# Sparse attention and FFN on one core: plain f32 loads with casts on the engines, attention spread by slots, a second output buffer, a fixed order for the first batch

## The chip, the cores and the metric

The kernel runs on one core of a Trainium2 chip. The metric is the device time of one execution in microseconds (us). The executions of one kernel that counted as fast agree within 1.5%: an execution further above the fastest of its kernel counts as slow, and fast runs are compared with fast runs alone. A median is of all runs of a kernel.

The engines of the core are TensorE (PE; its weight loads are listed as PEld), VectorE (DVE), ScalarE (ACT), GpSimd (POOL) and SyncE (SP, which here only issues transfers). Sixteen DMA engines move data between DRAM and the on-chip memory (SBUF). TensorE writes its results to PSUM.

The kernel before took 375.92 us (median of 4 runs, 373.97 to 377.35).

## The reference

The first part is an attention over 4 batches and 8 heads of 768 tokens with 64 elements each. A token sees its neighbours at a distance below 16, and beside them one summary of each block of 32 tokens: the maximum of the block's keys and the mean of its values. The second part is a feed-forward network (FFN) on the result, 3072 tokens of 512.

```python
k_sum = k.reshape(B, H, nb, block, D).max(axis=3)         # block = 32
v_sum = v.reshape(B, H, nb, block, D).mean(axis=3)
scores_l = scale * q @ k.T                                # kept where |i - j| < 16
scores_s = scale * q @ k_sum.T + log(block)
a = softmax(concat(scores_l masked, scores_s))
x = a @ concat(v, v_sum)                                  # then to (3072, 512)
h = x @ w_in                                              # 512 -> 2048
g = h * clip(h + 3, 0, 6) / 6
out = g @ w_out                                           # 2048 -> 512
```

(The code is abridged: names of axes and reshapes are left out.)

## The kernel before

The tokens are cut into 8 tiles of 384, two for each batch, and the heads are handled as 4 pairs (p). Stage s of the outer loop runs the attention of half batch s, the first FFN matmul (F1) of tile s-1 and the second (F2) of tile s-2. One stage has 16 slots: four F1 matmuls and three F2 matmuls each, with some steps of the attention in between. The order on TensorE is the program's. The other engines were ordered by the scheduler.

All of k, q, v and the weights came in bf16, by transfers that cast on the way and are issued by GpSimd. Only the rows for the block sums came as f32 from SyncE:

```python
def load_k(b, p):
    t = ld.tile([128, NT, 2, D], BF16, tag="kb", name="kb")
    for j in range(2):
        nc.gpsimd.dma_start(out=t[:, :, j], in_=k[b, 2 * p + j].rearrange("(s p) d -> p s d", p=128))
# ... the same for load_q and load_v, w_in and w_out in four chunks each
```

The transposes of keys and queries share one PSUM buffer. The key's transpose is read by two copies and the block maximum before the query's may overwrite it:

```python
ps_o = ctx.enter_context(tc.tile_pool(name="ps_o", bufs=1, space=PS))   # output of F2
ps_t = ctx.enter_context(tc.tile_pool(name="ps_t", bufs=1, space=PS))   # transposes
# ...
def Tk(b, p):
    tp = ps_t.tile([128, S], BF16, tag="t", name="tk")
    # ... 6 transposes
    nc.scalar.activation(t[0:64, :, 0:64], tp[0:64].rearrange(...), AF.Copy)
    nc.vector.tensor_copy(t[64:128, :, 64:128], tp[64:128].rearrange(...))
    nc.vector.reduce_max(red[:], tp[:].rearrange(...), axis=AX.X)
    nc.vector.tensor_tensor(kst[e][p]..., red..., hmk[:], op=ALU.mult)

def Tq(b, p, lo, hi):
    tp = ps_t.tile([128, S], BF16, tag="t", name="tq")
    # ... the transposes
    nc.vector.tensor_copy(qT[e][p][:, ...], tp[:, ...])
```

The scores are masked after the exponential, on DVE for batch 0 and on GpSimd later. GpSimd also makes the block sums of v for batches 1 to 3. Each half batch is one list of steps, and the even half carries all key work and the block sums of the batch:

```python
eng = nc.vector if b == 0 else nc.gpsimd
eng.tensor_tensor(a, a, mask[:].unsqueeze(1).to_broadcast([128, n, WIN]), op=ALU.mult)
# ...
T(0); T(1); L(0); T(2); L(1); A(0); T(3); L(2); A(1); L(3); A(2); A(3)
```

T stands for the transposes, L for scores and their exponential, A for the value step (numerator, denominator, and x = numerator times exp(-ln(denominator))). One slot of the FFN ends in a relu on ScalarE and a multiply on DVE that writes g:

```python
nc.scalar.activation(r[:], hp[:], AF.Relu, bias=half_c[:], scale=1.0 / 6.0)
nc.vector.scalar_tensor_tensor(gt[t][:, ft], r[:], 1.0, hp[:], op0=ALU.min, op1=ALU.mult)
```

The softmax here doesn't subtract the row's maximum and nothing guards it: scores larger than these inputs give would overflow.

Of the kernel before, what the change touches and what calls it, by code (L numbers as in the profile page):

```python
# [11 lines left out]
U32 = mybir.dt.uint32  # L12
# [5 lines left out]
D = 64  # L18
BLK = 32
# [7 lines left out]
def kernel(  # L27
# [19 lines left out]
    NTILE = B * 2  # L47

# [3 lines left out]
    ld = ctx.enter_context(tc.tile_pool(name="ld", bufs=5))  # L52
    vld = ctx.enter_context(tc.tile_pool(name="vld", bufs=1))
    work = ctx.enter_context(tc.tile_pool(name="work", bufs=2))
    xp = ctx.enter_context(tc.tile_pool(name="xp", bufs=3))
    gp = ctx.enter_context(tc.tile_pool(name="gp", bufs=2))
# [3 lines left out]
    ps_o = ctx.enter_context(tc.tile_pool(name="ps_o", bufs=1, space=PS))  # L60
    ps_t = ctx.enter_context(tc.tile_pool(name="ps_t", bufs=1, space=PS))
# [6 lines left out]
    kbd = [[const.tile([128, NK, 128], BF16, tag=f"kbd{e}{p}", name=f"kbd{e}{p}") for p in range(NP)] for e in range(2)]  # L68
    vbd = [[const.tile([128, NK, 128], BF16, tag=f"vbd{e}{p}", name=f"vbd{e}{p}") for p in range(NP)] for e in range(2)]
    qT = [[const.tile([128, S + 2 * HALO + 2], BF16, tag=f"qT{e}{p}", name=f"qT{e}{p}") for p in range(NP)] for e in range(2)]  # L70
    at = [[const.tile([128, NK, WIN], BF16, tag=f"at{e}{p}", name=f"at{e}{p}") for p in range(NP)] for e in range(2)]
    kst = [[const.tile([128, 128], BF16, tag=f"kst{e}{p}", name=f"kst{e}{p}") for p in range(NP)] for e in range(2)]
    vst = [[const.tile([128, 2, D], BF16, tag=f"vst{e}{p}", name=f"vst{e}{p}") for p in range(NP)] for e in range(2)]
    vfull = [vld.tile([128, BLK, D], F32, tag=f"vf{i}", name=f"vf{i}") for i in range(2)]
# [4 lines left out]
    kb_t, qb_t = {}, {}  # L79

    def load_k(b, p):
        t = ld.tile([128, NT, 2, D], BF16, tag="kb", name="kb")
        for j in range(2):
            nc.gpsimd.dma_start(out=t[:, :, j], in_=k[b, 2 * p + j].rearrange("(s p) d -> p s d", p=128))  # L84
        kb_t[b, p] = t

    def load_q(b, p):
        t = ld.tile([128, NT, 2, D], BF16, tag="qb", name="qb")
        for j in range(2):
            nc.gpsimd.dma_start(out=t[:, :, j], in_=q[b, 2 * p + j].rearrange("(s p) d -> p s d", p=128))  # L90
        qb_t[b, p] = t

    def load_v(b, p):
        t = vbd[b % 2][p]
        for j in range(2):
            nc.gpsimd.dma_start(  # L96
                out=t[j * 64:(j + 1) * 64, :, j * 64:(j + 1) * 64],
                in_=v[b, 2 * p + j].rearrange("(n p) d -> p n d", p=KB))

    def load_vfull(b, g):  # L100
        t = vfull[g]
        for j in range(2):
            src = v[b, 4 * g + 2 * j:4 * g + 2 * j + 2].rearrange("h (n t) d -> (h n) t d", t=BLK)
            nc.sync.dma_start(out=t[j * 64:j * 64 + 2 * NB], in_=src)
# [3 lines left out]


    for p in range(NP):  # L110
        load_k(0, p)
        load_q(0, p)
# [3 lines left out]
    identf = work.tile([128, 128], F32, tag="idf", name="identf")  # L116
    make_identity(nc, identf[:])
    nc.vector.tensor_copy(ident[:], identf[:])  # L118
    obd = const.tile([128, 2, D], BF16, tag="obd", name="obd")
    hmk = const.tile([128, 2, NB], BF16, tag="hmk", name="hmk")  # L120
    for t in (obd, hmk):
        nc.vector.memset(t[:], 0.0)
        nc.vector.memset(t[0:64, 0], 1.0)
        nc.vector.memset(t[64:128, 1], 1.0)

    def zero_off_diagonal(t):
        nc.vector.memset(t[0:64, :, 64:128], 0.0)
        nc.vector.memset(t[64:128, :, 0:64], 0.0)

    for e in range(2):  # L130
        for p in range(NP):
            zero_off_diagonal(kbd[e][p])
            zero_off_diagonal(vbd[e][p])
            nc.vector.memset(qT[e][p][:, 0:HALO], 0.0)
            nc.vector.memset(qT[e][p][:, S + HALO:], 0.0)
            nc.vector.memset(kst[e][p][:], 0.0)
    for g in range(2):
        nc.vector.memset(vfull[g][32:64], 0.0)
        nc.vector.memset(vfull[g][96:128], 0.0)
# [4 lines left out]
    for j in range(2):  # L144
        m = mask[j * 64:(j + 1) * 64]
        nc.gpsimd.affine_select(out=m, in_=m, compare_op=ALU.is_ge, fill=0.0, base=0,
                                channel_multiplier=-1, pattern=[[1, WIN]])
        nc.gpsimd.affine_select(out=m, in_=m, compare_op=ALU.is_ge, fill=0.0, base=2 * HALO,
                                channel_multiplier=1, pattern=[[-1, WIN]])

    hmv, osum = [], []
    for par in range(2):
        m = const.tile([128, 2, D], F32, tag=f"hmv{par}", name=f"hmv{par}")
        nc.gpsimd.memset(m[:], 1.0)
        for j in range(2):
            lo = 64 * par + NB * j
# [4 lines left out]
        o = const.tile([128, 2, D], BF16, tag=f"osum{par}", name=f"osum{par}")  # L161
# [4 lines left out]
    for g in range(2):  # L166
        load_vfull(0, g)
    for p in range(NP):
        load_v(0, p)
    for c in range(4):  # L170
        w = d_ff // 4
        nc.gpsimd.dma_start(out=w_in_sb[:, :, c * w:(c + 1) * w], in_=w_in_v[:, :, c * w:(c + 1) * w])
    for c in range(4):
        w = NFT // 4
        nc.gpsimd.dma_start(out=w_out_sb[:, c * w:(c + 1) * w], in_=w_out_v[:, c * w:(c + 1) * w])


    def vsum(b, g):
        eng = nc.vector if b == 0 else nc.gpsimd
        t = vfull[g]  # L180
        n = BLK // 2
        a = work.tile([128, n, D], F32, tag="va", name="va")
        eng.tensor_tensor(a[:], t[:, 0:n], t[:, n:2 * n], op=ALU.add)  # L183
        while n > 1:
            n //= 2
            eng.tensor_tensor(a[:, 0:n], a[:, 0:n], a[:, n:2 * n], op=ALU.add)  # L186
        for par in range(2):
            eng.tensor_tensor(vst[b % 2][2 * g + par][:], a[:, 0:1].to_broadcast([128, 2, D]), hmv[par][:], op=ALU.mult)
        if b + 1 < B:
            load_vfull(b + 1, g)  # L190


    asum, nd = {}, {}

    def Tk(b, p):
        e = b % 2
        src = kb_t[b, p][:].rearrange("p s h d -> p s (h d)")
        tp = ps_t.tile([128, S], BF16, tag="t", name="tk")
        for st in range(NT):
            nc.tensor.transpose(tp[:, st * 128:(st + 1) * 128], src[:, st], ident[:])  # L200
        t = kbd[e][p]
        nc.scalar.activation(t[0:64, :, 0:64], tp[0:64].rearrange("p (n c) -> p n c", c=KB), AF.Copy)  # L202
        nc.vector.tensor_copy(t[64:128, :, 64:128], tp[64:128].rearrange("p (n c) -> p n c", c=KB))
        red = work.tile([128, NB], BF16, tag="red", name="red")
        nc.vector.reduce_max(red[:], tp[:].rearrange("p (n c) -> p n c", c=BLK), axis=AX.X)  # L205
        off = 64 * (p % 2)
        nc.vector.tensor_tensor(
            kst[e][p][:, off:off + 2 * NB].rearrange("p (h n) -> p h n", h=2),
            red[:].unsqueeze(1).to_broadcast([128, 2, NB]), hmk[:], op=ALU.mult)

    def Tq(b, p, lo, hi):
        e = b % 2
        src = qb_t[b, p][:].rearrange("p s h d -> p s (h d)")
        tp = ps_t.tile([128, S], BF16, tag="t", name="tq")
        for st in range(lo, hi):
            nc.tensor.transpose(tp[:, (st - lo) * 128:(st - lo + 1) * 128], src[:, st], ident[:])  # L216
        nc.vector.tensor_copy(qT[e][p][:, HALO + lo * 128:HALO + hi * 128], tp[:, 0:(hi - lo) * 128])

    def Sl(b, p, lo, hi):
        e = b % 2  # L220
        n = hi - lo
        sp = ps_s.tile([128, 512], F32, tag="s", name="sl")
        for i in range(n):
            t = lo + i
            nc.tensor.matmul(sp[:, i * WIN:(i + 1) * WIN], kbd[e][p][:, t], qT[e][p][:, t * KB:t * KB + WIN],  # L225
                             start=True, stop=True)
        a = at[e][p][:, lo:hi]
# [4 lines left out]
    def Ss(b, g, half):  # L232
        e = b % 2
        sp = ps_s.tile([128, 512], F32, tag="s", name="ss")
        for par in range(2):
            p = 2 * g + par
            nc.tensor.matmul(sp[:, 0:HALF], kst[e][p][:], qT[e][p][:, HALO + half * HALF:HALO + (half + 1) * HALF],
                             start=(par == 0), stop=(par == 1))
        a = work.tile([128, HALF], BF16, tag="asum", name="asum")
        nc.scalar.activation(a[:], sp[:, 0:HALF], AF.Exp, scale=scl)  # L240
# [11 lines left out]
    def AVn(b, p, half):  # L252
        e = b % 2
        num = ps_n.tile([128, HALF], F32, tag="num", name="num")
        nd[b, p, half] = [num, None]
        bl = blocks_of(half)
        nc.tensor.matmul(num[:], vst[e][p][:].rearrange("p h d -> p (h d)"), asum[b, p // 2, half][:],  # L257
                         start=True, stop=False)
        for i, (t, lo, hi, off) in enumerate(bl):
            nc.tensor.matmul(num[:, lo:hi], vbd[e][p][:, t], at[e][p][:, t, off:off + hi - lo],  # L260
                             start=False, stop=(i == len(bl) - 1))

    def AVd(b, p, half, x):
        e = b % 2
        den = ps_n.tile([128, HALF], F32, tag="den", name="den")
        num = nd[b, p, half][0]
        a = at[e][p]
        ones = obd[:].rearrange("p h d -> p (h d)")
        nc.tensor.matmul(den[:], osum[p % 2][:].rearrange("p h d -> p (h d)"), asum[b, p // 2, half][:],
# [87 lines left out]
    for stage in range(NTILE + 2):  # L357
# [3 lines left out]
        if stage == 0:  # L361
            for st in steps:
                st()
# [44 lines left out]
```

## Time and profile before

| what | value |
|---|---|
| median of 4 runs | 375.92 us |
| profiled span | 376.5 us |
| PE busy | 255.8 us (68%) |
| DVE, ACT, POOL busy | 158.8, 157.2, 152.5 us (42, 42, 41%) |
| first FFN matmul | 65.9 us |
| TensorE's largest single wait on another engine after that | 16.2 us, for a mask on GpSimd |

The three engines beside TensorE are equally and lightly loaded on average, so averages tell little here. What matters is the table by stages, which the prediction below shows line by line: the start, the even stages, the tail. Its rows are cut at the first relu of each tile, except the first, which is cut at the first FFN matmul (66 us; the first relu is at 68.3).

### The profile page before, as it was taken

The numbers are of one execution on the slowest core, as the hardware profiler recorded it, in microseconds if no ns is written. First come the engines' busy times: TensorE is split into PE (matmuls) and PEld (weight loads), VectorE is DVE, ScalarE is ACT, GpSimd is POOL, SyncE is SP. The second block draws the span as 40 slices with busy tenths as digits, with TensorE's granted clock in tenths as the row PEclk, the third lists the DMA queues.
The fourth block names the chain that finished last, engine by engine and source line by source line (L and its number), as shares of the span: only waits on it lengthen the run. The fifth ranks groups of instructions, "written<-read, shape, count | busy, mean of one in ns | idle before, by whom it ended". The sixth has DMA issues, their size and how long they took to land.

```text
span 376.5 us, 4613 instructions
## 1 busy us (share of the span) xinstructions
PE 255.8 (68%) x1696; PEld 143.2 (38%) x1696; DVE 158.8 (42%) x336; ACT 157.2 (42%) x297; POOL 152.5 (41%) x203
## 2 busy tenths in 40 slices
PE   0000257886670179898857798989477989899985
PEld 0000234453340135454424454545244545454432
DVE  7475852465461042433454334334543343343310
ACT  1000234476250035556615455656254656564421
POOL 8992102899999933276334032520020302200000
PEclk9999999999798559999978899999788999999999
DMA  9999999997997660197763001900000000001011
GB/s 76 92 107 191 187 183 203 146 136 109 133 145 69 42 42 30 34 106 72 70 40 25 28 30 31 89 28 17 13 0 30 29 29 29 28 14 43 30 56 56
DMA packets 83990, 26.51 MB, mean 70 GB/s; under 512 B 76032, under 2 KB 80128, under 8 KB 83200
## 3 DMA queue, kind: packets, MB, share of 16 engines
q0 software_dynamic: 79488, 13.64, 47.5%
q1 hardware_dynamic: 4480, 12.59, 14.2%
q8 instruction: 13, 0.21, 0.3%
q14 instruction: 9, 0.07, 0.1%
HBM read 33.55 MB, written 6.29 MB: 106 GB/s over the span
## 4 chain that ended last, share of the span: by engine, by line
PE 54%; POOL 16%; ACT 10%; DMA 9%; DVE 6%; issue 4%; POOLq 0%; ACTq 0%
PE hp L334 21%; PE op L348 20%; DMA wout<-in_moe_w_out_dram 9%; POOL vbd L96 3%; POOL va L186 3%; ACT ot L352 3%; POOL qb L90 3%; POOL kb L84 3%; POOL va L183 2%; DVE red L205 2%; PE num L260 2%; PE num L257 2%; ACT kbd L202 2%; PE sl L225 2%; PE tq L216 2%
## 5 line engine op out<-in xcount | busy, mean ns | idle before, releaser
L348 PE MATMUL op<-wout,g 128*128 128x512 bf16 x384 | 110.8, 399 | 13.9 <-ACT ot L352 13.7
L334 PE MATMUL hp<-x,win 128*128 128x384 bf16 x512 | 115.3, 351 | 1.6 <-DVE g L338 0.8
L338 DVE SCALAR_TENSOR_TENSOR g<-r,hp 128x384 bf16<-128x384 f32 x128 | 70.7, 553 | 103.6 <-ACT r L337 103.0
L337 ACT ACTIVATE r<-hp,half_c 128x384 f32<-128x384 f32 x128 | 73.8, 577 | 85.4 <-PE hp L334 83.5
L230 POOL TENSOR_TENSOR at<-at,mask 128x376 bf16<-128x376 bf16 (+2 forms) x36 | 30.2, 843 | 105.7 <-ACT at L228 105.7
L334 PEld LDWEIGHTS <-win 128*128 128x128 bf16 x512 | 48.5, 104 | 30.5 <-issue 8.2
L348 PEld LDWEIGHTS <-g 128*128 128x128 bf16 x384 | 39.4, 103 | 49.2 <-issue 20.1
L216 PE MATMUL tq<-ident,qb 128*128 128x128 bf16 x96 | 12.8, 255 | 55.1 <-DVE red L205 53.2
L284 DVE TENSOR_TENSOR x<-num,lg 128x384 bf16<-128x384 f32 x32 | 17.9, 558 | 59.1 <-ACT lg L283 59.0
L90 POOL DMA_DIRECT2D qb<-in_q_dram x32 | 27.0, 864 | 31.7 <-PE tq L216 19.5
L84 POOL DMA_DIRECT2D kb<-in_k_dram x32 | 27.2, 867 | 27.5 <-DMA win<-in_moe_w_in_dram 12.4
L228 ACT ACTIVATE at<-sl 128x376 bf16<-128x376 f32 (+2 forms) x48 | 22.9, 483 | 27.0 <-PE sl L225 26.7
L282 ACT ACTIVATE lg<-den 128x384 f32<-128x384 f32 x32 | 15.6, 489 | 43.7 <-PE den L277 36.1
L216 PEld LDWEIGHTS <-qb 128*128 128x128 bf16 x96 | 7.9, 110 | 63.3 <-issue 61.0
L202 ACT ACTIVATE kbd<-tk 64x768 bf16<-64x768 bf16 x16 | 12.8, 802 | 43.9 <-PE tk L200 43.5
L260 PEld LDWEIGHTS <-vbd 128*128 128x128 bf16 x224 | 13.9, 104 | 32.6 <-issue 27.6
L260 PE MATMUL num<-at,vbd 128*128 128x94 bf16 (+2 forms) x224 | 15.1, 210 | 16.3 <-POOL at L230 16.3
L96 POOL DMA_DIRECT2D vbd<-in_v_dram x32 | 24.6, 781 | 3.7 <-DMA wout<-in_moe_w_out_dram 3.5
L200 PE MATMUL tk<-ident,kb 128*128 128x128 bf16 x96 | 10.0, 254 | 20.1 <-DVE ident L118 15.8
L352 ACT ACTIVATE ot<-op 128x512 f32<-128x512 f32 x24 | 14.2, 592 | 11.6 <-PE op L348 11.2
L225 PEld LDWEIGHTS <-kbd 128*128 128x128 bf16 x192 | 15.0, 115 | 9.9 <-issue 4.0
L225 PE MATMUL sl<-qT,kbd 128*128 128x94 bf16 x192 | 17.9, 231 | 0.0
(63 smaller groups left out, 233.7 us busy)
## 6 DMA issues: line engine op xcount, KB each, us to landing
vf<-in_v_dram SPq DMA_DIRECT2D x16, 384.0 KB, 7.5
out_dram<-ot SPq DMA_DIRECT2D x24, 256.0 KB, 2.0
kb<-in_k_dram POOLq DMA_DIRECT2D x32, 96.0 KB, 3.4
qb<-in_q_dram POOLq DMA_DIRECT2D x32, 96.0 KB, 3.4
vbd<-in_v_dram POOLq DMA_DIRECT2D x32, 96.0 KB, 3.4
win<-in_moe_w_in_dram POOLq DMA_DIRECT2D x4, 512.0 KB, 21.3
wout<-in_moe_w_out_dram POOLq DMA_DIRECT2D x4, 512.0 KB, 35.1
```

What stands on the lines that cost most here:

```text
L84: nc.gpsimd.dma_start(out=t[:, :, j], in_=k[b, 2 * p + j].rearrange("(s p) d -> p s d", p=128))
L90: nc.gpsimd.dma_start(out=t[:, :, j], in_=q[b, 2 * p + j].rearrange("(s p) d -> p s d", p=128))
L96: nc.gpsimd.dma_start(out=t[j * 64:(j + 1) * 64, :, j * 64:(j + 1) * 64], in_=v[b, 2 * p + j].rearrange("(n p) d -> p n d", p=KB))
L216: nc.tensor.transpose(tp[:, (st - lo) * 128:(st - lo + 1) * 128], src[:, st], ident[:])
L225: nc.tensor.matmul(sp[:, i * WIN:(i + 1) * WIN], kbd[e][p][:, t], qT[e][p][:, t * KB:t * KB + WIN], start=True, stop=True)
L230: eng.tensor_tensor(a, a, mask[:].unsqueeze(1).to_broadcast([128, n, WIN]), op=ALU.mult)
L260: nc.tensor.matmul(num[:, lo:hi], vbd[e][p][:, t], at[e][p][:, t, off:off + hi - lo], start=False, stop=(i == len(bl) - 1))
L334: nc.tensor.matmul(hp[:], w_in_sb[:, kt, ft * 128:(ft + 1) * 128], xt[t][:, kt], start=(kt == 0), stop=(kt == NP - 1))
L337: nc.scalar.activation(r[:], hp[:], AF.Relu, bias=half_c[:], scale=1.0 / 6.0)
L338: nc.vector.scalar_tensor_tensor(gt[t][:, ft], r[:], 1.0, hp[:], op0=ALU.min, op1=ALU.mult)
L348: nc.tensor.matmul(ops[t][:], gt[t][:, ft, ts * 128:(ts + 1) * 128], w_out_sb[:, ft], start=(ft == 0), stop=(ft == NFT - 1))
L352: nc.scalar.activation(o[:], ops[t][:], AF.Copy)
```

## The change

The intent is to take the issuing of transfers from GpSimd, to break up the serial chains of the even stages, and to start the FFN earlier. Its parts are these.

- All transfers are plain f32, issued by SyncE. The casts to bf16 are instructions on DVE, and on ScalarE for half of the weights and part of the first batch.
- The attention of a whole batch is spread over the 32 slots of two FFN stages. Batch 1 is packed into stages 0 and 1, batches 2 and 3 into stages 2 and 3 and stages 4 and 5. F2 lags F1 by two tiles.
- The transposes lose their own PSUM buffer and take turns in pools of two that others use too; F2's output has two buffers in place of one. In batches 0 and 1 every second numerator and denominator uses the output's buffers (`alt`).
- The first batch has a fixed order on ScalarE, DVE and GpSimd.
- Smaller parts: one set of tiles for the keys, queries, values and exponentials where there was one for even and one for odd batches; one buffer more for x and for g; block sums on 96 rows in place of 128, those of the first batch on GpSimd; for the later batches both copies of a key's transpose on ScalarE; and copies out of the transposes that write every second element.

```diff
-        nc.gpsimd.dma_start(out=t[:, :, j], in_=k[b, 2 * p + j].rearrange("(s p) d -> p s d", p=128))
+    for n, src in (("k", k), ("q", q)):
+        t = ld.tile([128, NT, 2 * D], F32, tag=n + "f", name=n + "f")
+        nc.sync.dma_start(out=t[:], in_=src[b, 2 * p:2 * p + 2].rearrange("h (u p s) d -> p (h u) (s d)", p=128, s=2))
+    ...
+    copy = nc.scalar.copy if b == 0 and n == "q" else nc.vector.tensor_copy
+    copy(t[:, :, :, j], r[:, :, j])
-    ps_o = ctx.enter_context(tc.tile_pool(name="ps_o", bufs=1, space=PS))
-    ps_t = ctx.enter_context(tc.tile_pool(name="ps_t", bufs=1, space=PS))
+    ps_o = ctx.enter_context(tc.tile_pool(name="ps_o", bufs=2, space=PS))
+    alt = b < 2 and p % 2 == 1
+    pool = ps_o if alt else ps_n
-        T(0); T(1); L(0); T(2); L(1); A(0); T(3); L(2); A(1); L(3); A(2); A(3)
+            quad = [(0, lambda p=pa: Tk(b, p)), (1, lambda p=pa: Tq(b, p)),
+                    (2, lambda p=pb: Tk(b, p)), (3, lambda p=pb: Tq(b, p)),
+                    ...
+                    (9, lambda p=pa: AV(b, p, 0)), (11, lambda p=pb: AV(b, p, 0)),
+                    (13, lambda p=pa: AV(b, p, 1)), (15, lambda p=pb: AV(b, p, 1))]
+            steps += [(start + int((o + s) * scale), f) for s, f in quad]
+    start = tc.manual_schedule(engines={ET.Activation, ET.DVE, ET.Pool})
+    ...  (the first batch, in order)
+        start, scale = (8, 0.75) if b == 1 else (32 * (b - 1), 1)
```

(The loads of v and the weights change in the same way.)

## The prediction

> **What bounds the kernel now.** I read first the forty slices, then the busy time stage by stage, then the waits of the slow stages, then the chain that ended last. In the page's slices (a digit is tenths busy, a slice 9.4 us):
>
> ```profile
> PE   0000257886670179898857798989477989899985
> PEclk9999999999798559999978899999788999999999
> DMA  9999999997997660197763001900000000001011
> q0 software_dynamic: 79488, 13.64, 47.5%
> q1 hardware_dynamic: 4480, 12.59, 14.2%
> ```
>
> TensorE does almost nothing for four slices while the DMA engines are full; counted from 0, there is a hole in slices 12 and 13, and the clock falls there and near slices 20 and 28. The last two lines say which queue holds the DMA engines: the casting loads from GpSimd. I cut the span where the first of each 16 relu evictions starts (ScalarE line 337), so each row is one stage of the loop (columns: start:end, length, then busy time of PE, weight loads, DVE, ACT, POOL, then clock, DMA share, GB/s):
>
> ```profile
> 0.00:66.00 66.00, 15.87 (x121) 11.17 (x122) 39.98 (x111) 11.31 (x21) 34.08 (x60) 1.00 1.33 148
> 66.00:91.50 25.50, 21.35 (x151) 12.53 (x149) 14.09 (x29) 15.93 (x32) 23.60 (x29) 1.00 1.49 136
> 91.50:156.30 64.80, 37.45 (x232) 20.35 (x231) 22.77 (x36) 21.61 (x41) 46.26 (x56) 0.76 0.76 70
> 156.30:186.60 30.30, 27.06 (x193) 15.22 (x193) 11.66 (x24) 17.59 (x34) 18.51 (x24) 1.00 0.89 79
> 186.60:232.10 45.50, 34.49 (x232) 19.35 (x232) 19.09 (x36) 21.50 (x41) 11.00 (x14) 0.89 0.25 31
> 232.10:262.40 30.30, 27.05 (x193) 15.21 (x193) 11.65 (x24) 17.57 (x34) 9.02 (x10) 1.00 0.38 47
> 262.40:307.50 45.10, 34.05 (x233) 19.02 (x233) 19.08 (x36) 21.45 (x42) 6.05 (x8) 0.89 0.05 18
> 307.50:337.80 30.30, 27.08 (x193) 15.25 (x193) 11.66 (x24) 17.60 (x34) 3.99 (x4) 1.00 0.08 27
> 337.80:360.00 22.20, 20.54 (x108) 10.51 (x108) 8.31 (x15) 10.21 (x18) 0.00 (x0) 1.00 0.10 37
> 360.00:376.50 16.50, 10.85 (x49) 4.58 (x47) 0.55 (x1) 2.39 (x4) 0.00 (x0) 1.00 0.17 64
> ```
>
> There are three losses: 66 us before the first FFN matmul; even stages of 45 us (the first 65 us) against odd ones of 30 us; and 22 + 16.5 us at the end, where TensorE is the bound. The waits and the chain say why:
>
> ```profile
> PE tq L216 <- DVE red L205: 53.2, 16, 17.7
> PE num L260 <- POOL at L230: 16.3, 2, 16.2
> PE op L348 <- ACT ot L352: 13.7, 17, 0.9
> 27.94 32.92 DMA wout<-in_moe_w_out_dram
> ```
>
> First line: the query transposes wait for the key's reduce, because one PSUM buffer serves both, 16 times. Second: in the 65 us stage the mask multiply stood on GpSimd behind loads and block sums (its timeline there is full from 108 to 130 us), and TensorE waited 16.2 us at once. Third: one output PSUM buffer, some 0.8 us at each of 17 evictions. Fourth: on the chain of the start, 33 us are a weight transfer.
>
> **What the Trainium skill says.** "DMA: Bandwidth & Descriptors", section "SWDGE vs HWDGE vs iDMA": a load that casts must be issued from GpSimd, whose cores make the descriptors; plain ones go from SyncE and take nothing from GpSimd. The trace agrees: 96 K/Q/V issues of some 840 ns are GpSimd time (27.2 + 27.0 + 24.6 us); a SyncE issue of the same size is 0.32 us. "TensorE: Matmul & The Clock Gate", section "Part 1": after idleness the array runs at half clock. Here, four FFN matmuls are 0.81 us in the undisturbed stage but 1.48 us after the 16 us hole. "VectorE: DVE Perf Modes", section "The perf-mode tier table": an fp32 copy between SBUF tiles runs two elements a cycle. No such big copy is in this trace; the bf16 copy from PSUM (561 ns for 768 elements) has that rate. "SBUF — State Buffer", section "Who interferes with whom": such a copy, and a DVE operation with two SBUF inputs, block against GpSimd for a whole instruction. Here the 128x48 multiply that writes kst takes 183 ns in the median and 3895 ns once, with GpSimd busy. The change adds many such copies.
>
> **The change, part by part.**
> (1) Loads. All come from SyncE as f32. Bytes landed rise from 26.5 MB to 40 MB (q, k, v, and v again, 6.29 MB each, 8.4 MB weights, 6.29 MB out), but rows become longer: 512 B for q and k. Rates, as estimates from the page: q0's 79488 packets share 47.5% of 16 x 376.5 us, 36 ns each; q1's 4480 share 14.2%, 191 ns for 2.8 KB, which is 236 GB/s. At 36 ns a packet on 16 engines, 512 B rows give 227 GB/s and 256 B rows (v) 114. Batch 0 in the order of SyncE's queue: q and k 3.15 MB 13.9 us, v rows 1.57 MB 6.7, v 1.57 MB 13.8, first w_in chunk 1.05 MB 4.4: 39 us, and 2.5 for start and landing, 41 us. The chain of compute beside it: ScalarE's fixed list for batch 0 has about 38 instructions at 0.5 to 1.0 us (8 query casts, 8 PSUM copies of 0.8, 12 exponentials of 0.48, 4 vbd casts, logs), 27 us, from 6 us on, plus some 6 us of waits for DVE and TensorE: about 40 us. So the first FFN matmul comes at **43 us in place of 66: -23**.
> (2) Stages 0 and 1 (32 FFN1 slots, rest of batch 0, all of batch 1, no FFN2). ScalarE: 32 relu at 0.65 us (start to start when back to back) 20.8, kbd 8 x 0.80, exponentials 12 x 0.5, sums 6 x 0.5, logs 24 x 0.52, weight casts 7 x about 1.05: 56 us. DVE: 32 x 0.57 for g, 12 x 0.56 for x, 16 q/k casts of 384 at about 0.36, 8 v casts of 768 at 0.56, qT, reduces, weight casts 7 x 0.7: 48 us, and some 6 of blocking. TensorE: about 38 us. DMA has 65 us of work after the first w_in chunk at the rates above (w_in 13.3, batch 1 34.4, w_out 17.8). All are near 55 to 65 in dependent order: **67 us**. Before, the two stages with this FFN1 work took 25.5 + 64.8 = 90.3 us; they held half of batch 1 less, and one FFN2 (48 matmuls at 0.217, 10.4 us) more, which after lies in the tail.
> (3) Stages 2 to 5, two pairs with one batch each. TensorE at full clock: a slot of 4 + 3 matmuls is 1.30 us (the undisturbed stage repeats every 1.29 to 1.30), 32 slots 41.6. Attention of one batch, from start-to-start times in warm stretches: 8 value steps (a head pair's numerator and denominator for one half) x 0.84, 48 score matmuls x 0.04, 8 block-sum scores x 0.16, 48 transposes x 0.055: 6.7 + 1.9 + 1.3 + 2.6 = 12.5. So 54 us. By the durations of (2), ScalarE needs 47 (relu 20.8, kbd 6.4, exponentials 8, logs 8.3, evictions 3.6) and DVE 41 (g 18.2, x 4.5, casts 10.3, qT and reduces 7.6) plus blocking. What goes: the transposes now lie a slot apart and use two buffers, so the 2.5 us wait per head is over other work, and GpSimd has no issues, so no mask waits. What comes: bursts of two kbd copies (1.6 us) or four casts (1.4 us) before a relu or g, while only two hp buffers give about 0.5 to 1 us of slack: about 8 stalls of 1 us. A pair is **62 us, two are 124**; before it was 75.8 and 75.4.
> (4) Stages 6 and 7: pure FFN, 32 x 1.30 = 41.6, with two output buffers no eviction wait: **42.5**.
> (5) Tail: FFN2 lags two stages, so 96 matmuls at 0.217 (16 took 3.63 us, less 0.38 of the last's own latency, by 15) are 20.8; last eviction and store as before, 3.5: **24.3** in place of 16.5.
> Sum: 43 + 67 + 124 + 42.5 + 24.3 = **301**; several terms were rounded upwards, so I put **298 us**.
>
> **Rivals.** *ScalarE and DVE become the bound everywhere*: for it, 87% and 76 to 87% of the ideal pair; against it, evictions can be delayed a little without TensorE stopping. Then pairs cost 70 and stages 0 and 1 75: about 322 us. *DMA becomes the bound of stages 0 and 1*: 40 MB, SyncE's queue in order, so a load waiting for its buffer holds all behind it, and DVE's casts of batch 2 stand before the g of stage 2. For it, the DMA row of before is full to 85 us; against it, no descriptors from GpSimd and 2 KB rows. It would add 10 to 20 us: 310 to 318. *Everything hides*: first matmul at 38, stages 0 and 1 at 56, pairs at 57, 276 us. *The cost only moves, no gain*: this needs 80 us of new stalls; the FFN content, about 166 us at 1.30 per slot, does not change, and nothing speaks for it.
>
> **Range and chances.** The ends of the range are the second and the third rival with small luck: **276 to 322**, eight in ten. Faster by over 2% is below 369.6 us, 70 us away: 0.97. Within 2%: 0.02. Slower: 0.01.
>
> **What would show it.** First FFN matmul at 39 to 47 us; the first FFN2 at 100 to 118; pairs of 57 to 68 us with no wait of TensorE over 3 us and a clock of 0.95 or more after 110 us; no GpSimd issues; 42 to 44 us for the two pure stages; 96 matmuls in one run at the end. I am wrong if the first w_in chunk lands after 50 us, if TensorE's longest waits are for DMA after 60 us, or if relu or g wait queues make pairs of over 70 us.

## The result

The changed kernel took **296.46 us** (median of 4 runs, 294.99 to 298.65) and is correct. Its ratio to the kernel before is 0.789, with a 95% interval of 0.7825 to 0.7963. Ratios here are the mean time of one kernel's fast runs over the mean of the other's fast runs of the same rounds, so they are not quite the ratio of the medians. The profiled execution has a span of 295.4 us, at a mean clock of 0.96.

Slices of the changed kernel, 7.4 us each (digits as before), and its only busy DMA queue:

```profile
PE   0533868749969497799859998999999999999995
POOL 8885000595234019660293075400420000000000
PEclk9999999966999969999986999999999999999999
DMA  8999949992860999664874770011100101001211
q1 hardware_dynamic: 58752, 39.85, 53.5%
```

TensorE starts early and is nearly full from slice 21 on. The queue of casting loads is gone. The DMA row is full at the start, again in slices 13 to 15, and stays half busy up to slice 23. The clock row still dips, now in slices 8 and 9, 14 and 20 to 21.

The stages, cut at the first relu of each tile (columns as in the prediction; the border of stages 0 and 1 lies one relu, some 0.46 us, too early, here and in the stages of the other runs):

```profile
0.00:42.65 42.65, 18.37 (x154) 13.67 (x155) 29.86 (x71) 26.18 (x45) 23.27 (x43) 1.00 0.97 229
42.65:73.04 30.39, 22.66 (x179) 14.33 (x178) 27.00 (x40) 22.67 (x41) 14.40 (x15) 0.83 0.97 220
73.04:98.97 25.93, 21.70 (x203) 13.93 (x201) 23.16 (x45) 23.66 (x45) 8.38 (x12) 1.00 0.50 159
98.97:137.43 38.46, 31.56 (x215) 17.85 (x215) 28.96 (x51) 24.22 (x43) 18.02 (x20) 0.91 0.86 195
137.43:172.40 34.97, 30.88 (x214) 17.32 (x213) 23.55 (x40) 21.61 (x41) 12.26 (x14) 0.90 0.70 180
172.40:201.95 29.55, 27.95 (x214) 16.29 (x213) 21.05 (x38) 21.63 (x40) 11.71 (x13) 1.00 0.24 55
201.95:230.63 28.68, 27.80 (x214) 16.48 (x213) 14.28 (x26) 21.60 (x40) 4.89 (x6) 1.00 0.08 29
230.63:251.09 20.46, 20.46 (x112) 10.80 (x111) 9.33 (x17) 10.86 (x21) 0.00 (x0) 1.00 0.09 33
251.09:271.90 20.81, 20.81 (x113) 10.89 (x112) 8.86 (x16) 10.87 (x19) 0.00 (x0) 1.00 0.10 38
271.90:295.40 23.50, 19.98 (x93) 8.88 (x91) 0.00 (x0) 3.58 (x6) 0.00 (x0) 1.00 0.21 79
```

The same TensorE work, 214 instructions and one batch's share of attention, takes 38.5 and 35.0 us in stages 2 and 3 and only 29.6 and 28.7 in stages 4 and 5. In the latter TensorE is busy for 95 to 97% of the stage. So the schedule itself fits, and something else costs stages 2 and 3 some 15 us more (73.4 against 58.2). Of these, 6.7 us are TensorE's own busy time (62.4 against 55.8 us), at a clock of 0.91 and 0.90 in place of 1.00. The rest is idle time. Stages 2 and 3 differ from 4 and 5 in their DVE busy time (52.5 against 35.3 us), GpSimd (30.3 against 16.6) and the DMA load: besides their own batch, they also take the loads and casts that prepare the next.

The waits (in all, times, longest; us) that answer to those of before:

```profile
PE tp L210 <- DVE kb L126: 19.8, 4, 7.9
PE hp L303 <- DVE g L307: 11.3, 9, 3.2
...
PE tp L210 <- DVE red L220: 1.2, 5, 0.5
```

The wait for the key's reduce fell from 53.2 us, of which 26.8 lay after the first FFN matmul, to 1.2. The wait for the output's eviction (13.7 us) and that for the mask (16.3) are not in the list any more. New is the wait for a cast of keys. Most of it lies in the start: 7.9 us are the very first transpose, which waits for the first key. The wait of F1 for g, 0.8 us in all before, is 11.3 now.

The terms of the prediction beside what was measured:

| term | before | predicted | measured |
|---|---|---|---|
| start | 66.0 | 43 | 42.65 (first FFN matmul at 40.1) |
| stages 0 and 1 | 90.3 | 67 | 56.3 |
| stages 2 and 3 | 75.8 | 62 | 73.4 |
| stages 4 and 5 | 75.4 | 62 | 58.2 |
| stages 6 and 7 | (before, one such stage: 22.2) | 42.5 | 41.3 |
| tail | 16.5 | 24.3 | 23.5 |
| sum | (stages hold other work before) | 301, put at 298 | 295.4 |

The total is nearly right because an error of -11 us in stages 0 and 1 and one of +11 us in stages 2 and 3 cancel. That is luck. The experiments had to explain both the large gain and these two errors.

One stretch of stage 2 shows what the list of waits only hints at. It is the timeline of the changed kernel (start, duration, engine, line, instruction, count; in brackets the idle time before it and what ended it), of DVE, GpSimd and TensorE:

```profile
115.63 2.00 DVE L126 CAST qb<-qf 128x384 bf16<-128x384 f32 x2
...
119.37 1.90 DVE L126 CAST qb<-qf 128x384 bf16<-128x384 f32 x2
...
116.39 5.57 POOL L241 TENSOR_TENSOR at<-at,mask 128x376 bf16<-128x376 bf16 x6
...
121.79 0.81 PE L303 MATMUL hp<-x,win 128*128 128x384 bf16 x4 [1.86 <-DVE g L307]
```

Two pairs of query casts take 2.00 and 1.90 us while GpSimd multiplies six masks from 116.4 to 122.0 us. Each cast takes 0.99 to 1.08 us, about as long as one mask (0.95 us). Earlier in the same trace, with GpSimd idle, such a pair takes 0.62 to 0.63 us (at 102 to 107 us). The g behind the casts is late, and TensorE stands still for 1.86 us.

### The profile page after: what moved, and what is told of

Its sections match the earlier page's. It is cut to its first block, busy times and chain, and to the rows that moved or that the text cites. A ratio compares the mean times of both kernels' runs of the same rounds, so it can differ in the third digit from the quotient of the medians.

```text
span 295.4 us, 4629 instructions
## 1 busy us (share of the span) xinstructions
PE 242.2 (82%) x1696; PEld 140.4 (48%) x1696; DVE 186.1 (63%) x341; ACT 186.9 (63%) x333; POOL 92.9 (31%) x121
## 4 chain that ended last, share of the span: by engine, by line
PE 53%; DVE 25%; ACT 12%; DMA 4%; issue 4%; SPq 1%; ACTq 0%
PE op L313 23%; PE hp L303 19%; ACT kbd L217 4%; DVE red L220 4%; DVE g L307 4%; DVE kst L222 3%; DVE kb L126 3%; DVE qb L126 3%; DMA kf<-in_k_dram 2%; PE num L275 2%; DMA qf<-in_q_dram 2%; PE tp L210 2%; DVE vbd L131 2%; DVE qT L229 2%; ACT r L306 2%
## 5 line engine op out<-in xcount | busy, mean ns | idle before, releaser
L303 PE MATMUL hp<-x,win 128*128 128x384 bf16 x512 | 108.1, 336 | 12.7 <-DVE g L307 11.3
L313 PE MATMUL op<-wout,g 128*128 128x512 bf16 x384 | 101.0, 386 | 0.2 <-ACT lg L291 0.2
L306 ACT ACTIVATE r<-hp,half_c 128x384 f32<-128x384 f32 x128 | 72.6, 578 | 40.1 <-PE hp L303 39.1
L307 DVE SCALAR_TENSOR_TENSOR g<-r,hp 128x384 bf16<-128x384 f32 x128 | 69.7, 549 | 42.4 <-ACT r L306 42.1
L241 POOL TENSOR_TENSOR at<-at,mask 128x376 bf16<-128x376 bf16 x36 | 32.8, 935 | 52.0 <-ACT at L239 51.4
L195 POOL TENSOR_TENSOR va<-vr 96x1024 f32<-96x1024 f32 x8 | 18.9, 2364 | 66.9 <-DMA vr<-in_v_dram 66.9
L217 ACT COPY kbd<-tp 64x768 bf16<-64x768 bf16 x28 | 28.3, 1009 | 12.7 <-PE tp L210 12.3
L210 PE MATMUL tp<-ident,kb 128*128 128x128 bf16 x96 | 9.6, 247 | 22.9 <-DVE kb L126 19.8
L239 ACT ACTIVATE at<-sl 128x376 bf16<-128x376 f32 x48 | 21.4, 483 | 6.5 <-PE sl L236 6.1
L317 ACT ACTIVATE ot<-op 128x512 f32<-128x512 f32 x24 | 14.2, 593 | 17.6 <-PE op L313 17.2
L198 POOL TENSOR_TENSOR va<-va 96x512 f32<-96x512 f32 (+3 forms) x32 | 24.3, 760 | 2.3
L236 PEld LDWEIGHTS <-kbd 128*128 128x128 bf16 x192 | 12.7, 111 | 19.0 <-issue 14.5
L220 DVE TENSOR_REDUCE red<-tp 128x24 bf16<-128x768 bf16 x16 | 15.2, 952 | 7.0 <-ACT kbd L217 6.9
L292 ACT ACTIVATE lg<-lg 128x384 f32<-128x384 f32 x32 | 16.7, 523 | 0.9
L126 DVE CAST kb<-kf 128x384 bf16<-128x384 f32 x32 | 15.9, 530 | 1.3 <-DMA kf<-in_k_dram 1.3
```

The source lines that it names most:

```text
L126: copy(t[:, :, :, j], r[:, :, j])
L198: eng.tensor_tensor(a[:, 0:n], a[:, 0:n], a[:, n:2 * n], op=ALU.add)
L210: nc.tensor.transpose(tp[:, s, u * 128:(u + 1) * 128], t[:, s, u].rearrange("p h d -> p (h d)"), ident[:])
L217: copy(kbd[p][rows, :, 64 * j:64 * j + 64].rearrange("p n (c s) -> p s n c", s=2), tp[rows].rearrange("p s (n c) -> p s n c", c=KB // 2))
L220: nc.vector.tensor_reduce(red[:], tp[:].rearrange("p s (n c) -> p n s c", c=BLK // 2), axis=AX.XY, op=ALU.max)
L236: nc.tensor.matmul(sp[:, i * WIN:(i + 1) * WIN], kbd[p][:, t], qT[p][:, t * KB:t * KB + WIN], start=True, stop=True)
```

## The experiments

All twelve ran in three groups. The runs of one group shared a chip and the runs of the kernel before, whose medians were 374.6 to 375.0 us. Ratios are to the kernel before, so the changed kernel's own 0.789 (0.7825 to 0.7963) is the mark. "Stages" are lengths cut at the first relu of each tile, of one profiled execution. The start took 43.5 to 45.0 us in e3, e7 and e9, which do not change it (42.65 in the changed kernel), so a difference of some 2 us in a single stage says little. The letters A, B, C, D and A2 name theories. A is that the plain loads pay for themselves, and B that they do not matter. C is that stages 2 and 3 are long because SyncE's queue is held up by a weight load. D is that DVE and GpSimd block each other there. A2 is that the later batches would be better off with GpSimd's loads.

### e1: q, k and weights as casting loads again

```diff
-            nc.sync.dma_start(out=t[:], in_=src[b, 2 * p:2 * p + 2].rearrange(...))      # f32
+                nc.gpsimd.dma_start(out=t[:, :, :, j], in_=src[b, 2 * p + j].rearrange(...))   # casts to bf16
-            copy(w_in_sb[...], t[...])                                              # DVE and ScalarE
+        nc.gpsimd.dma_start(out=w_in_sb[:, :, c * w:(c + 1) * w], in_=w_in_v[:, :, c * w:(c + 1) * w])
```

(The casts of q and k fall away, w_out likewise; v stays as changed. The bf16 tiles of q and k get four buffers in place of two.)

> The changed kernel, but q, k and both weights come again as casting loads from GpSimd (v stays as changed); the slots and the fixed order stay. Theory A (the plain loads are a cause of the gain of their own): GpSimd gets 64 issues of some 0.85 us and 8 for the weights, about 60 us of work before its masks and block sums; the first FFN matmul moves from 41 us to 55 or later, masks come late again, and the time is 315 to 340 us. Rival B (the slots alone make the gain, loads are hidden anyway; and DVE is freed of 56 casts): 290 to 302 us.

Measured: 311.87 us, ratio 0.832 (0.8265 to 0.8368), correct. The start is 59.9 us in place of 42.65 and stage 0 is 40.8 in place of 30.4, but stages 2 and 3 together are 58.2 us in place of 73.4. The start and stage 2 of this run (columns as above):

```profile
0.00:59.87 59.87, 20.52 (x153) 14.52 (x154) 30.59 (x61) 21.87 (x36) 55.00 (x79) 1.00 1.48 186
...
128.96:157.94 28.98, 27.79 (x210) 16.63 (x214) 18.71 (x32) 21.64 (x39) 18.89 (x22) 1.00 0.67 86
```

GpSimd is busy for 55.0 of the first 59.9 us. So the plain loads are worth 17.2 us at the start and 10.4 in stage 0, of which about 15 are given back in stages 2 and 3. The net is 15.4 us (311.87 less 296.46). Theory A has the right direction, with a smaller size than expected.

### e2: a fourth staging buffer

```diff
-    big = ctx.enter_context(tc.tile_pool(name="big", bufs=3))
+    big = ctx.enter_context(tc.tile_pool(name="big", bufs=4))
```

In the changed kernel SyncE waits 17.4 us, once, for a staging buffer of w_out, and the loads of batch 2 stand behind it in its queue.

> The changed kernel with four instead of three staging buffers for weights and v rows. Theory C (stage 2 is late because the fourth w_out load waits 17.4 us for a staging buffer and holds batch 2's k and q behind it in SyncE's queue): the first k of batch 2 is issued near 80 us instead of 95.9, the casts of batch 2 no longer wait, and 4 to 8 us go: 288 to 292 us. Rival D (stage 2 is slow by the blocking between DVE and GpSimd, not by the loads): under 2 us.

Measured: 296.65 us, ratio 0.791 (0.7863 to 0.7965). The wait of 17.4 us is gone and the first key of batch 2 is requested at 77.1 us in place of 95.9. Yet stages 2 and 3 are 40.3 and 32.1 us, together 72.3. The first key cast starts no earlier, at 104.1 us in place of 102.3, and takes longer: the block sums of batch 2 come earlier too (101.3 us in place of 109.9) and now run beside the casts. DVE and GpSimd in e2:

```profile
100.77 3.43 DVE L116 CAST wout<-wo 128x1024 bf16<-128x1024 f32 x2
104.12 2.21 DVE L126 CAST kb<-kf 128x384 bf16<-128x384 f32 x2
...
101.30 2.35 POOL L195 TENSOR_TENSOR va<-vr 96x1024 f32<-96x1024 f32 x1 [9.39 <-DMA vr<-in_v_dram]
103.72 3.31 POOL L198 TENSOR_TENSOR va<-va 96x512 f32<-96x512 f32 x4
```

In the changed kernel the same two pairs of casts took 1.28 and 0.63 us. TensorE's wait for a key cast in these stages grew from 3.1 to 6.2 us. So the late transfer is real, and making it early alone brings nothing. What the lateness costs without this collision e2 does not show. In e3 below, where the first key of batch 2 is requested as late and GpSimd is idle, that wait is 3.0 us. So theory C explains at most a small part of the 15 us.

### e3: no mask and no block sums on GpSimd

```diff
+        if b > 0:
+            return                      # no mask for batches 1 to 3
-                vsum(b, g)
```

> The changed kernel without GpSimd's block sums and mask multiplies for batches 1 to 3: a wrong result on purpose. Theory D (DVE's casts and its small multiply stand still[...]): the q/k casts on DVE fall from a mean of 530 to 575 ns to about 350, the kst multiply from 748 to about 180, and the time falls by 10 to 18 us: 278 to 287 us, mostly in stages 0 to 3. Rival (bursts of work in front of a relu or g stop TensorE, whoever is next to it): under 4 us.

Measured: 282.69 us, ratio 0.751 (0.7458 to 0.757); one of the four runs was slow. The result is wrong (relative error 1.12). The groups of casts on DVE (busy us, mean ns), first of the changed kernel, then of this run:

```profile
L126 DVE CAST kb<-kf 128x384 bf16<-128x384 f32 x32 | 15.9, 530 | 1.3 <-DMA kf<-in_k_dram 1.3
L126 DVE CAST qb<-qf 128x384 bf16<-128x384 f32 x24 | 12.9, 575 | 0.7 <-DMA qf<-in_q_dram 0.7
```

```profile
L126 DVE CAST kb<-kf 128x384 bf16<-128x384 f32 x32 | 11.8, 404 | 1.1 <-DMA kf<-in_k_dram 1.1
L126 DVE CAST qb<-qf 128x384 bf16<-128x384 f32 x24 | 7.5, 352 | 2.0 <-DMA qf<-in_q_dram 2.0
```

The query casts fell from a mean of 575 ns to 352. Stages 2 and 3 took 62.6 us, 10.8 fewer, and DVE was busy for 42.8 us in them in place of 52.5, at the same number of instructions (91). TensorE's two longest groups of waits in these stages of the changed kernel, then the same two of this run:

```profile
PE hp L303 <- DVE g L307: 5.8, 3, 3.2
PE tp L210 <- DVE kb L126: 3.1, 1, 3.1
...
PE tp L210 <- DVE kb L126: 3.0, 1, 3.0
PE hp L305 <- DVE g L309: 0.3, 1, 0.3
```

The wait for g fell by 5.5 us, and TensorE's busy time by 5.3 (62.4 to 57.2 us, at a clock of 0.97 in place of 0.91). These two make up the 10.8 us. Whether the clock was lower because of the stalls was not tested. Stage 0 was 5.4 us shorter. The cause in stage 0 can be seen on one instruction. The timeline of the changed kernel:

```profile
61.09 5.29 DVE L222 TENSOR_TENSOR kst<-red,hmk 128x48 bf16<-128x48 bf16 x1
...
61.53 4.81 POOL L241 TENSOR_TENSOR at<-at,mask 128x376 bf16<-128x376 bf16 x6
...
66.89 1.44 PE L303 MATMUL hp<-x,win 128*128 128x384 bf16 x4 [2.80 <-DVE g L307]
```

A tiny multiply of two SBUF operands lasts 5.29 us and ends with GpSimd's run of six masks (at 66.38 and 66.34 us). In this experiment the same instruction at the same place takes 0.17 us. This agrees with the Trainium skill, page "SBUF — State Buffer", section "Who interferes with whom", by which such an operation contends with GpSimd's reads. It also shows a size the page doesn't give: the loser waited for a run of instructions.

What follows: GpSimd's work beside DVE's costs about 14 us in this kernel (296.46 less 282.69), 10.8 of them in stages 2 and 3. Theory D holds for the size of this loss. The run removes the masks' and sums' own dependences too, so it is an upper bound on the blocking, but TensorE waited for neither masks nor sums in the changed kernel's list.

### e4: the first batch in the scheduler's order

```diff
-    start = tc.manual_schedule(engines={ET.Activation, ET.DVE, ET.Pool})
-    start.__enter__()
...
-    start.__exit__(None, None, None)
```

> The changed kernel with the first batch's ScalarE, DVE and GpSimd work left to the scheduler instead of the fixed order. If the fixed order matters: the first FFN matmul is 5 us or more later than 41 us, the time over 301 us. If the loads alone set the start: the first FFN matmul within 2 us of 41, the time within 1% of 296.

Measured: 307.09 us, ratio 0.817 (0.8113 to 0.823). The start is 47.9 us, 5.3 longer, stage 1 is 32.6, 6.7 longer (at a clock of 0.84 in place of 1.00), and the rest differs by little. The fixed order is worth 10.6 us, half of it at the start.

### e5 and e6: casting loads for the later batches only

e5 keeps the plain loads for batches 0 and 1 and the weights, and gives q and k of batches 2 and 3 to casting loads from GpSimd. e6 does the same and also takes the masks of batch 1 from GpSimd to DVE. In both, the bf16 tiles of q and k get four buffers in place of two.

```diff
+        if b >= 2:       # e5 and e6: q and k
+            nc.gpsimd.dma_start(out=t[:, :, :, j], in_=src[b, 2 * p + j].rearrange(...)); return
-        eng = nc.vector if b == 0 else nc.gpsimd     # e6: masks
+        eng = nc.vector if b < 2 else nc.gpsimd
```

> The changed kernel, with q and k of batches 2 and 3 alone loaded as casting transfers from GpSimd (32 issues), everything of the start and the weights as changed. Theory A2 (from the run with all q, k and weight loads on GpSimd: plain loads win at the start and lose in stages 2 and 3, where their 32 casts stand on DVE in front of g and are blocked by GpSimd): the first FFN matmul stays near 41 us, stages 2 and 3 fall from 38.5 + 35.0 us to about 29 + 29, and the time is 279 to 285 us. Rival (stages 2 and 3 were short in that run only because everything was later and its data had long been there): 292 to 297 us.

> The same, and batch 1's 12 mask multiplies on DVE instead of GpSimd. If the 5.3 us for which DVE's small kst multiply stood behind six masks in stage 0 is on the path: another 3 to 6 us less than the hybrid, 274 to 281 us. If DVE is too full there (12 multiplies of about 0.45 us more): no gain or 2 us more.

e5 measured 297.88 us (294.32 to 299.3). Only two of its four runs counted as fast, and no interval was given, so it is only said to be no gain that can be seen. Theory A2 falls. Its stages 2 and 3 are 37.0 and 31.4 us. DVE has fewer casts, but GpSimd still holds it up. The timelines of DVE and GpSimd in e5:

```profile
110.74 3.94 DVE L231 TENSOR_TENSOR kst<-red,hmk 128x48 bf16<-128x48 bf16 x1
...
109.50 2.76 POOL L86 DMA_DIRECT2D kb<-in_k_dram  x2
111.24 3.39 POOL L204 TENSOR_TENSOR va<-vr 96x1024 f32<-96x1024 f32 x1
```

The multiply ends with GpSimd's addition, at 114.68 and 114.63 us, and not with the issues. TensorE's next F1 matmul waited 6.41 us for the g behind that multiply.

e6 measured 289.82 us (286.95 to 291.09), ratio 0.772 (0.7665 to 0.7771), correct. The interval lies below the changed kernel's, so this version is about 2.2% faster (0.7718 over 0.7894), though the two did not run in the same rounds. Its stages 2 and 3 are 31.3 and 32.6 us, 63.9 together. It is the best correct version, and it is still above the 274 to 281 us that the blocking theory allowed.

### e7: the attention packed into half the slots

```diff
-        start, scale = (8, 0.75) if b == 1 else (32 * (b - 1), 1)
+        start, scale = (8, 0.75) if b == 1 else (32 * (b - 1), 0.5)
```

> The changed kernel with the attention of batches 2 and 3 packed into 16 slots in place of 32. If the spread itself is worth much: stages 2 and 4 rise to 48 to 52 us, stages 3 and 5 fall to 21, the sum of the four rises from 132 to 140 or more, 304 us or more. If only the order (transposes a slot apart, two buffers) counts, not the density: within 3 us of 296.

Measured: 311.90 us, ratio 0.829 (0.8225 to 0.8358). Stages 2 to 5 are 56.7, 21.0, 44.2 and 20.5 us, 142.4 in all in place of 131.7. Stage 4 looks like an even stage of before again (45 us), stage 2 is longer, and 3 and 5 are nearly pure FFN. One of the four runs was slow. By the fast ones the spreading is worth 14 to 15 us (mean 310.9 less 296.6; the ratios say 15).

### e8 and e12: one output buffer, and no alternate buffers

In the changed kernel the output's two buffers serve two ends: the F2 result, and every second numerator and denominator of batches 0 and 1. e12 takes away the second use. e8 takes away that and the second buffer, so e12 is e8's control.

```diff
-        alt = b < 2 and p % 2 == 1
+        alt = False                     # e8 and e12
-    ps_o = ctx.enter_context(tc.tile_pool(name="ps_o", bufs=2, space=PS))
+    ps_o = ctx.enter_context(tc.tile_pool(name="ps_o", bufs=1, space=PS))     # e8 only
```

> The changed kernel with one output buffer in PSUM instead of two (and batches 0 and 1 without the alternate buffers for numerator and denominator, which need it). If the second buffer is worth what the waits of before say (13.7 us at 17 evictions of 24): TensorE waits 0.7 us at each of 24 evictions, some 16 us, of which those in stages 2 to 5 may lie beside other stalls: 304 to 314 us. If evictions are hidden: under 4 us more.

> The changed kernel without the alternate numerator and denominator buffers for batches 0 and 1, two output buffers kept: the control for the run with one output buffer (320.2 us). If that run's loss is the output buffer's, this one is within 4 us of 296, and stages 6 and 7 keep 20.5 us each. If it is the alternate buffers': 305 us or more, with the loss before stage 2.

e8 measured 320.17 us, ratio 0.853 (0.8472 to 0.8578). e12 measured 306.41 us, ratio 0.808 (0.8012 to 0.8147); two of its four runs were slow, and the fast ones took 302.54 and 303.88 us. The waits of e8, then of e12:

```profile
PE op L313 <- ACT ot L317: 15.2, 18, 1.0
```

```profile
PE num L273 <- DVE x L293: 14.8, 12, 1.9
```

Without the second buffer the wait of before (13.7 us, 17 times) is back. By fast runs the second buffer is worth 16 to 17 us (mean 319.7 less 303.2, across two groups; the ratios say 0.853 less 0.808, 17 us). Without the alternate buffers, numerators wait for the division before them. That is worth about 7 us by fast runs (303.2 less 296.6): the start is 48.8 us in place of 42.65.

e12 shows a thing that was not expected: its stages 2 and 3 are 31.7 and 30.1 us, 61.8 together, with all of GpSimd's masks and sums in place and the key casts at a mean of 576 ns in these stages. TensorE's clock there is 1.00, and six of the 24 casts of q and k had run before stage 2. Its execution up to the end of stage 3 is only 2.9 us longer than the changed kernel's (175.25 against 172.40), though its stage 2 begins 14.5 us later. So the blocking's 10.8 us is no fixed price. It may depend on how the bursts of masks fall against the casts and the g of the slots, which no run here varies alone.

### e9, e10 and e11: GpSimd's work moved to DVE

e9 moves the masks of batch 1 to DVE, e10 all masks. e11 moves all masks and, for batches 1 to 3, the block sums as one reduce, with four staging buffers.

```diff
-        eng = nc.vector if b == 0 else nc.gpsimd
+        eng = nc.vector if b < 2 else nc.gpsimd      # e9; e10 and e11: eng = nc.vector
+            eng.tensor_reduce(a[:, 0], t[0:RS].rearrange("p t d -> p d t"), axis=AX.X, op=ALU.add)   # e11
```

> The changed kernel with batch 1's 12 mask multiplies on DVE, loads as changed. If the gain of 7 us over the hybrid came from these masks[...]: stage 0 falls from 30.4 to about 25 us and the time to 287 to 292 us. If it needed the hybrid's loads: 294 to 298 us.

> The changed kernel with all mask multiplies on DVE; GpSimd keeps the block sums. Theory D says that most of the blocking goes: DVE does 36 more multiplies of 0.36 to 0.45 us (4.5 us a batch), and its casts come back to 350 to 450 ns; stages 2 and 3 fall from 73.5 to 64 to 68 us, the time to 281 to 287 us. If DVE's own load counts for more: 290 us or over.

> All masks, and the block sums of batches 1 to 3, as one reduce of 2048 elements each, on DVE, so that GpSimd is idle after the start; four staging buffers. Meant as a version that beats both: no blocking at all, DVE 9 us more work a batch. 277 to 284 us if blocking was the cost and DVE has room; 288 us or over if DVE becomes the bound in the stages with attention (a reduce of about 2.1 us stands in front of a g).

e9 measured 296.30 us (one of five runs was slow), ratio 0.786 (0.7792 to 0.792). Stage 0 fell by 4.8 us (25.6 in place of 30.4) as the blocking theory says, and stage 1 grew by 4.7 (30.6 in place of 25.9). In e9's stage 1 DVE is busier (26.0 against 23.2 us) and the clock is 0.89 in place of 1.00, while in stage 0 it is 0.93 in place of 0.83. So the low clock moved from one stage to the next. What sets its moment was not tested.

e10 measured 294.02 us (one of four runs was slow), ratio 0.782 (0.7771 to 0.7875): at most a little faster, far from the 281 to 287 expected. Its profile fell into a slow execution and isn't compared here.

e11 measured 297.67 us, ratio 0.795 (0.7889 to 0.8002). GpSimd is idle after the start, and the key casts are back at a mean of 403 ns, so the blocking is gone. DVE pays for it with its own work:

```profile
L197 DVE TENSOR_REDUCE vd<-vr 96x64 f32<-96x2048 f32 x6 | 21.8, 3631 | 0.0
```

I had guessed 2.1 us for one such reduce. It took 3.6, and a g behind it comes late in the same way. So e11 removes the blocking, and e9 in stage 0, but the totals stay near the changed kernel's. In e11 the moved work is seen to cost DVE time. For e10 this is not shown.

## Why the prediction was right, and where it was wrong

**The start (43 predicted, 42.65 measured; first FFN matmul at 40.1).** This was right as a whole, and its mechanism is shown: with casting loads it is 59.9 us (e1), in the scheduler's order 47.9 (e4), without the alternate buffers 48.8 (e12). The prediction counted only the loads and the order and did not know the worth of the alternate buffers. Of its two paths, the transfers (41 us) were put too long: the first chunk of w_in landed at 32.6 us. The prediction took 36 ns for each packet of 256 or 512 B, where the changed kernel's took 26.5 and 32.0 ns on average, and the core moved 229 GB/s through the whole start. So the other path, the chain of compute put at 40 us, set the start.

**Stages 0 and 1 (67 predicted, 56.3 measured).** The step that failed is to take three sums of 48 to 65 us as a chain "in dependent order", all of them but DVE's too large. The DMA sum of 65 us measured 42.4 (0.97 of 30.4 and 0.50 of 25.9 us): two of its chunks of w_in had landed in the start, one of w_out came later, and packets were faster than taken. The ScalarE sum of 56 us measured 46.3 us busy. The relu was put at its start-to-start time of 0.65 us, where 0.577 each was used (17.8 in place of 20.8); of the seven weight casts only four fell into these stages (4.2 us in place of 7.35); the kbd copies were larger than taken (1.0 us each, 8.0 in place of 6.4). These durations overlap at their ends, which takes off the rest. The DVE sum, 48 and 6 of blocking, was nearer (50.2 busy), so DVE and not ScalarE was the fuller engine. The two stages took 56.3 us, 6 more than DVE was busy, so the three overlapped.

**Stages 2 to 5 (62 each; measured 73.4 and 58.2).** The mechanism of the gain was right: the transposes' wait fell from 53.2 to 1.2 us, the masks hold up nothing, and packing the attention again gives back about 15 us (e7). The step that failed is "DVE needs 41 plus blocking", where blocking got no size of its own in these stages, and the "about 8 stalls of 1 us". In stages 2 and 3 DVE was busy for 52.5 us, and TensorE's clock fell to 0.91 and 0.90 on top. Without GpSimd's work the pair took 62.6 us (e3), near the predicted 62. So the term that was mis-sized is the blocking: given no size, it was 10.8 us in this phase of the schedule, half as longer waits for g and half as TensorE's lower clock. One of the prediction's own signs of being wrong came true here, a pair of over 70 us with waits for g. The rival of ScalarE and DVE as the bound everywhere is wrong, as stages 4 and 5 show. Its 70 us is near stages 2 and 3, but these engines were busy for only 45.8 and 52.5 us there. The rival of late loads foresaw 10 to 20 us, and the late key cast held TensorE for 3.1 us.

**Stages 6 and 7 and the tail (42.5 and 24.3; measured 41.3 and 23.5).** Right. The second output buffer keeps these stages free of the eviction wait; e8 and e12 put its worth in the whole kernel at 16 to 17 us, against the 13.7 us of waits seen before.

**The markers.** Right were the first FFN matmul, the absence of GpSimd issues, and the one run of F2 matmuls at the end. The first F2 matmul came at 99.1 us, just below its range of 100 to 118. The pure stages took 41.3 us, just below 42 to 44. The pairs were outside 57 to 68 once. The clock was 0.91 and 0.90 in stages 2 and 3 and TensorE's longest wait there was 3.2 us, so both of these markers were wrong: they rested on stages without stalls.

**Two slips without effect.** 2% below 375.92 us is 368.4 and not 369.6. The SyncE issue of 0.32 us was for 384 KB, where GpSimd's were 96 KB, so it was not "of the same size"; in the changed kernel SyncE's issues of loads took 0.45 to 1.18 us in the median.

**Where the gain came from.** 79.5 us in all (375.92 less 296.46). The single parts measure about 15 us for the plain loads net, 10.6 for the fixed order, about 7 for the alternate buffers, 16 to 17 for the second output buffer and 14 to 15 for the spreading, some 63 to 65 in sum. These were each taken out alone and need not add up. The rest, with the two transpose buffers among it, was not taken apart.

**What stays open.** e1 and e12 have short stages 2 and 3 although GpSimd works there. Whether that is the different timing of the masks, the data that is earlier relative to the stage, or fewer casts was not separated: e5 speaks against the casts alone; e2 does not decide on the data, as its earlier loads met more blocking. Why e6 gains where neither e5 nor e9 does is not settled either.

## What to carry to other kernels

Moving casts from the transfers to DVE frees GpSimd and shortens the start, but each cast between SBUF tiles is then an instruction that GpSimd's own work can hold up, so look at the median and the maximum of such an instruction, not at its mean, before trusting a sum of durations. A chain in which one buffer is written, read three times and written again shows in the list of waits beforehand (53.2 us here); a second buffer and a slot of distance together took nearly all of that away. When a total agrees with the prediction, check the terms: here two errors of 11 us cancelled.

## What the Trainium skill lacked or had wrong

- "SBUF — State Buffer", "Who interferes with whom": the page says the loser blocks for a whole instruction of the other. Here a 0.17 us multiply stood 5.29 us beside a run of six masks, so it lost to several instructions in a row, while casts beside such masks took 0.99 us each, about one mask (0.95 us). What happens beside such runs is lacking. The page infers that an operation with two SBUF inputs does not meet GpSimd's making of descriptors. In e5 such a multiply took 3.94 us beside two issues and an addition, and ended with the addition, which doesn't speak against that.
- "VectorE: DVE Perf Modes", "The perf-mode tier table": nothing wrong. The cast from f32 agrees with its 2× (341 to 360 ns for 384 elements without GpSimd's work).
- "ScalarE: Activation LUTs": no size for an output with a step. A copy of 768 bf16 elements from PSUM took 802 ns before and 1009 ns now, when it writes every second element. The instruction is also another one (COPY in place of ACTIVATE), so the step alone isn't shown to be the cause.
- "DMA: Bandwidth & Descriptors": no times by row size for plain loads on this chip. The changed kernel's packets took 26.5 ns at 256 B, 32.0 at 512 B, 92.6 at 2 KB and 528 at 8 KB on average. An estimate with one time for all small rows, as in the prediction, came out too slow.
